# Retention into a bilinear FFN on one core: the SP queue, one stretch and two copies of the opening blocks in another order

## The chip, the cores and the metric

The kernel runs on one core of a Trainium2 chip. The metric is device time in microseconds (us). Seven runs of the kernel before gave a median of 334.33 us, from 333.03 to 336.23. One further execution was taken with the hardware profiler: it took 333.72 us, 332.0 of them inside the profiled span, at a granted TensorE clock of 1.0.

## The reference

Two stages, of which the second eats the first:

```
scores = (q @ k^T) / sqrt(64)                 # per batch (8) and head (8), 576 x 576
ret    = scores * gamma[h] ** (i - j)  for i >= j, else 0,   gamma[h] = 1 - 2 ** (-5 - h)
attn   = ret @ v                              # 8 x 8 x 576 x 64
x      = attn with heads side by side         # 4608 tokens x 512
out    = ((x @ w_a) * (x @ w_b)) @ w_out      # 512 -> 1536 -> 512, float32
```

There is no softmax, so the retention is computed block by block with running states (sums of k^T v), and the powers of gamma are folded into v (factor gamma^-j) and into the result (factor gamma^i).

## The kernel before, in words

**Pairs of key tiles.** The 4608 tokens are cut into 18 pieces of 256 tokens, called pairs here. Pairs 0 to 2 are worked in two halves of four heads each ("steps", lines 281 to 421) with transposes on TensorE. Pairs 3 to 17 are worked whole by these functions:

- `load_pair(n)` (line 134) issues six loads on SP's queue: two each of q, k and v, 256 KB each, in rows of 64 floats (256 bytes). Each of the three goes to a tile of the pool `stage`, which has four buffers for each of q, k and v.
- `ahead(n)` (line 433) turns q and k to bf16 on GpSimd (POOL) with three copies each (lines 440 and 444) and then scales v (line 445).
- `turn(n)` (line 466) issues two transposing DMAs on SP's queue (line 471), one for q and one for k. Pair 3 alone is transposed on TensorE (`turned`).
- `stretch(into, outof)` (line 620) is TensorE's share of retention, four runs of 32 small products, about 0.3 to 0.4 us each: for the pair `outof`, results from the states (line 589); for the pair `into`, its own k^T v (line 506) and its scores (line 563), which need the transposed tile; then, again for `outof`, results from the keys (line 602). The work that follows on VectorE (DVE) and ScalarE (ACT) is put into the list `later` and handed out one piece at a time by `pop()`: sums of states (lines 523 and 526), their bf16 copies (lines 530 to 537), the scaling of the result into x (line 612) and the masking of the scores (line 572). A stretch first flushes what is left in `later`. The result tile and the score tile of a stretch have one PSUM buffer each, so a stretch can't write them before the DVE work of the one before has read them.

**The FFN.** `ffn_block` (line 667) runs over blocks of tokens: 512, 256, 256 and then seven of 512. For each of the 12 slices of the hidden width it makes four products with `w_a` (line 682), copies the sum to bf16 on ACT (line 690), makes four products with `w_b` (line 697) and multiplies on DVE (line 702). Then, for every 128 tokens, 12 products with `w_out` (line 716), a copy of the sum from PSUM to a tile `osb` in SBUF (line 725 on ACT, line 727 on DVE), and a store of it. All PSUM tiles of the FFN, and two of a stretch, come in turn from one pool of four buffers (`ps_ffn`), and `osb` comes in turn from four buffers. So the copy of the sixth 128 tokens goes to the buffer of the second 128 tokens, and it needs the stores of the second to have landed. The tokens of pairs 0 to 2 are stored by two DMAs of 64 rows each (line 653).

**Who sets the order.** The schedule is written by hand. A list `todo` (lines 838 to 862) holds functions with due times, counted in products of 512 columns: the first block lasts from 0 to 144, the next two from 144 to 216 and from 216 to 288. The generator of the FFN yields the cost of each product, and an entry is called at the first allowed place ("edge") at or after its due time; in the output products these places are every four products. Each engine then works through its own queue strictly in order. SP's queue carries all q, k and v loads, all transposing DMAs and all stores, so each of them stands behind whatever was issued before it.

The parts of the order that the change touches are, in SP's queue before: the six loads of pair 5; the two stores of the first 128 tokens; the transposes of pair 4; the six stores of the other 384 tokens of the first block; the four loads of q and k of pair 6; the transposes of pair 5; the two loads of v of pair 6; two stores; the transposes of pair 6.

Of the kernel before, what the change touches and what calls it, by code (L numbers as in the profile page):

```python
# [18 lines left out]
def kernel(  # L19
# [27 lines left out]
    FIRST = 3  # L47
# [3 lines left out]
    def regular(n):  # L51
        return n - (n > NP - 3)
# [4 lines left out]
    def rows_of(n):  # L57

        if n not in LEFT:
            m = regular(n)  # L60
            return [(kp, 0, 128, m // 2, 256 * (m % 2) + 128 * kp)
                    for kp in (0, 1)]
        return [(i // 2, 64 * (i % 2), 64, 4 * LEFT[n] + i, S - 64)
                for i in range(4)]
# [43 lines left out]
    def x_of(t0, n):  # L108

        b0 = 0  # L110
        for n_b in blocks:
            if t0 < b0 + n_b:
                break
            b0 += n_b
        if b0 not in x_tiles:
            x_tiles[b0] = x_pool.tile([128, HP, 512], BF16, tag="x", name="xT")
        return x_tiles[b0][:, :, t0 - b0:t0 - b0 + n]
# [14 lines left out]
    paired = {}  # L132

    def load_pair(n, which=(0, 1, 2)):
        if n >= NP:
            return
        paired.setdefault(n, [])
        for i in which:
            name, src = (("qf", q), ("kf", k), ("vf", v))[i]
            t = stage.tile([128, 2 * DM], FP32, tag=name, name=name + "2")  # L140
            for kp, r0, m, b, s0 in rows_of(n):
                nc.sync.dma_start(
                    t[r0:r0 + m, kp * DM:(kp + 1) * DM]
                    .rearrange("p (h d) -> p h d", h=H),
                    src[b, :, s0:s0 + m, :].rearrange("h s d -> s h d"))
            paired[n].append(t)

    def load_step(n, hh, which):

        if n not in paired:  # L150
            paired[n] = [stage.tile([128, 2 * DM], FP32, tag=name, name=name)
                         for name in ("qf", "kf", "vf")]
        nc.sync.dma_start(
            paired[n][which][:, hh * DM:(hh + 1) * DM]
            .rearrange("p (h e) -> p h e", h=4),
            (q, k, v)[which][n // 2, 4 * hh:4 * hh + 4,
                             256 * (n % 2):256 * (n % 2) + 256, :]
            .rearrange("h (p two) d -> p h (two d)", two=2))

    STEPS = [(0, 0), (1, 0), (0, 1), (1, 1), (2, 0), (2, 1)]  # L160
    Q, K, V = 0, 1, 2
# [105 lines left out]
    def pop():  # L267
        if later:
            later.pop(0)()
# [163 lines left out]
    def ahead(n):  # L433


        qf, kf, vf = paired.pop(n)
        qkb = nat.tile([128, 2, 2 * DM], BF16, tag="qkb", name="qkb2")
        vb = nat.tile([128, 2 * DM], BF16, tag="vb", name="vb2")
        for w, t in ((0, qf), (1, kf)):
            nc.gpsimd.tensor_copy(qkb[0:64, w], t[0:64])  # L440
            to = qkb[64:128, w].rearrange("p (j r d) -> p j r d", r=2, d=D)
            fro = t[64:128].rearrange("p (j r d) -> p j r d", r=2, d=D)
            for r in (0, 1):
                nc.gpsimd.tensor_copy(to[:, :, 1 - r], fro[:, :, r])  # L444
        nc.gpsimd.tensor_tensor(  # L445
            vb.rearrange("p (k h d) -> p k h d", k=2, h=H),
            vf.rearrange("p (k h d) -> p k h d", k=2, h=H),
            vs2[:, 2 if n in LEFT else regular(n) % 2].unsqueeze(3).to_broadcast([128, 2, H, D]),
            op=ALU.mult)
        natural[FIRST + n, "pair"] = (qkb, vb)  # L450
# [194 lines left out]
    def store(u, cols, osb):  # L645
        n, u = place(u // 2), u % 2
        for kp, r0, m, b, s0 in rows_of(n):
            rows = out[b * S + s0:b * S + s0 + m, cols]
            if kp != u:
                continue  # L650
            if n < FIRST:
                for par in (0, 1):
                    nc.sync.dma_start(rows[par::2], osb[half(par), cols])  # L653
            else:
                nc.sync.dma_start(rows, osb[r0:r0 + m, cols])
# [11 lines left out]
    def ffn_block(tb, tok0, n, runs):  # L667

        xT = x_of(tok0, n)
        hT = h_pool.tile([128, NF, 512], BF16, tag="h", name="hT")  # L670
        f0 = 0
        for count in runs:
            has = {}
            for F in range(f0, f0 + count):
                fs = slice(F * 128, (F + 1) * 128)
                pa = (begun[F] if tb == 0 and F in begun else
                      ps_ffn.tile([128, 512], FP32, tag="ab", name="pa"))
                for c in range(NC):
                    if tb == 0 and (F, c) in begun:
                        yield n / 512, False  # L680
                        continue
                    nc.tensor.matmul(pa[:, 0:n], wa_sb[:, c, fs],  # L682
                                     xT[:, c],
                                     start=(c == 0), stop=(c == NC - 1))
                    if c < NC - 1:
                        yield n / 512, False
                if n == 512 and tb:
                    pop()
                ha = ha_pool.tile([128, 512], BF16, tag="ha", name="ha")
                nc.scalar.copy(ha[:, 0:n], pa[:, 0:n])  # L690
                has[F] = ha
                yield n / 512, False
            for F in range(f0, f0 + count):
                fs = slice(F * 128, (F + 1) * 128)
                pb = ps_ffn.tile([128, 512], FP32, tag="ab", name="pb")
                for c in range(NC):
                    nc.tensor.matmul(pb[:, 0:n], wb_sb[:, c, fs],  # L697
                                     xT[:, c],
                                     start=(c == 0), stop=(c == NC - 1))
                    if c < NC - 1:  # L700
                        yield n / 512, False
                nc.vector.tensor_tensor(hT[:, F, 0:n], has[F][:, 0:n],  # L702
                                        pb[:, 0:n], op=ALU.mult)
                pop()
                yield n / 512, True
            f0 += count
        for u in range(n // 128):
            final = tok0 + (u + 1) * 128 == NTOK
            osb = o_pool.tile([128, DM], FP32, tag="osb", name="osb")
            for part in range(2 if final else 1):  # L710
                cols = (slice(part * DM // 2, (part + 1) * DM // 2) if final
                        else slice(0, DM))
                po = ps_ffn.tile([128, 512], FP32, tag="ab", name="po")
                width = cols.stop - cols.start
                for F in range(NF):
                    nc.tensor.matmul(po[:, 0:width],  # L716
                                     hT[:, F, u * 128:(u + 1) * 128],
                                     wo_sb[:, F, cols],
                                     start=(F == 0), stop=(F == NF - 1))
                    if F in (2, 5, 8):  # L720
                        pop()
                    if F < NF - 1:
                        yield width / 512, F % 4 == 3
                if (u + part) % 2 == 0:
                    nc.scalar.copy(osb[:, cols], po[:, 0:width])  # L725
                else:
                    nc.vector.tensor_copy(osb[:, cols], po[:, 0:width])  # L727
                store(tok0 // 128 + u, cols, osb)
                pop()
                yield width / 512, True  # L730
# [75 lines left out]
    nc.sync.dma_start(gate, wo_sb[0:1, 3, 0:64])  # L806
    for i, which in ((4, Q), (4, K), (4, V), (5, Q), (5, K), (5, V)):
        load_step(*STEPS[i], which)
    for n in range(FIRST, FIRST + 3):
        load_pair(n)  # L810

# [20 lines left out]
    def turn_step(i):  # L834
# [3 lines left out]
    todo = [(8, state_step, (1, (1,))), (20, state_step, (3, (1,))),  # L838
            (100, early_casts, ()), (112, turn_step, (4,)),
            (112.1, cast_step, (5, Q, "act")), (116, score_step, (4,)),  # L840
            (124, turn_step, (5,)), (124.1, state_step, (4, (0, 1))),
            (128, score_step, (5,)), (132, output_step, (4,)),
            (132.1, state_step, (5, (0, 1))), (140, output_step, (5,))]
    todo += [(28 + 6 * step, pair_tables, (step,)) for step in range(13)]
    todo += [(170, stretch, (3, None)), (197, stretch, (4, 3)),
             (246, stretch, (5, 4)), (280, stretch, (6, 5)),
             (372, stretch, (7, 6)), (408, stretch, (8, 7))]
    for n in range(8, NP, 2):
        todo += [(starts[n] - 116, stretch, (n + 1, n)),
# [3 lines left out]
    casts = {3: 104, 4: 104.1, 5: 143, 6: 200, 7: 250, 8: 330}  # L853
    turns = {4: 104.2, 5: 151, 6: 210, 7: 338, 8: 345}
    loads = {7: 212, 8: 271, 9: 345.1, 10: 345.2}
    todo += [(150, load_pair, (6, (0, 1))), (152, load_pair, (6, (2,)))]
    for n in range(9, NP):
        casts[n], turns[n] = placed[n] - 70, placed[n] - 38
    todo += [(156 + 3 * part, turned, (3, part)) for part in range(4)]
# [45 lines left out]
```

## Time and profile before

| what | value |
|---|---|
| median of 7 runs | 334.33 us |
| the profiled execution | 333.72 us, span 332.0 us |
| TensorE products (PE) | 319.5 us busy, 96% of the span |
| DVE, ACT, POOL | 163.8, 128.4 and 114.6 us busy |
| DMA | 50.37 MB in 143175 packets, mean 152 GB/s |
| queue q1 (SP's) | 138384 packets, 45.10 MB, 65.2% of 16 engines |
| block 0 (512 tokens), from its first product to its last output product | 18.2 to 54.0 us |
| blocks 1 and 2 (256 tokens each) | 54.0 to 73.7 and 73.7 to 93.7 us |
| block 3 begins | 95.03 us |

Times inside the profile are microseconds from the span's start. A line of a timeline gives start, length, engine, line of the kernel, operation, output and inputs; "x4" is how many instructions were merged into it, and a bracket at its end says how long the engine sat idle before it and who released it. For SP's queue the length is that of issuing, not of the transfer; the time from issue to landing is asked for separately. The releaser of a wait is inferred: when the engine named was done long before, it was another, often a DMA.

### The profile page before, as it was taken

To read this page: it belongs to the slowest core of one execution; us is meant where nothing else is said; L and a number is where in the kernel's file an instruction comes from. 1 tells how busy PE (TensorE), PEld (TensorE's weight loads), DVE (VectorE), ACT (ScalarE), POOL (GpSimd) and SP (SyncE) were. 2 spreads that over 40 slices of the span, in tenths; PEclk is the share of its full clock that TensorE was granted. 3 is DMA by queue.
4 is the path that set the end of the run, shared out by engine and by line. 5 is a ranking of instruction groups with operands and counts; after the bars stand their busy time and mean duration, and the time that the engine had idled before them with its cause. 6 is when DMAs were issued, how large, how long until landed. Compare 5 with 4: busy or idle time off the path is not lost.

```text
span 332.0 us, 8671 instructions
## 1 busy us (share of the span) xinstructions
PE 319.5 (96%) x3612; PEld 167.8 (51%) x3648; DVE 163.8 (49%) x292; ACT 128.4 (39%) x275; POOL 114.6 (35%) x146
## 2 busy tenths in 40 slices
PE   8999999989989999999999999999999999999996
PEld 4644457858634554545454545454445444444443
DVE  6744445664673465656265625662456246414321
ACT  7725833553533344343235313532332333213321
POOL 4960178725258277356054505360430000000000
PEclk9999999999999999999999999999999999999999
DMA  7999999979999999994599258945850420031013
GB/s 216 251 186 207 262 227 210 204 155 219 160 206 254 222 198 217 223 213 94 138 226 208 64 128 185 220 77 149 179 118 4 137 55 0 2 95 34 1 27 100
DMA packets 143175, 50.37 MB, mean 152 GB/s; under 512 B 124576, under 2 KB 138656, under 8 KB 143136
## 3 DMA queue, kind: packets, MB, share of 16 engines
q1 hardware_dynamic: 138384, 45.10, 65.2%
q0 software_dynamic: 4752, 4.72, 8.8%
q8 instruction: 28, 0.46, 0.6%
q14 instruction: 11, 0.09, 0.1%
HBM read 37.75 MB, written 9.44 MB: 142 GB/s over the span
## 4 chain that ended last, share of the span: by engine, by line
PE 90%; DMA 4%; DVE 2%; issue 2%; SPq 1%; ACT 1%; POOL 0%; ACTq 0%; DVEq 0%; POOLq 0%
PE pb L697 27%; PE po L716 27%; PE pa L682 26%; PE o L589 2%; PE o L602 1%; DMA vf<-in_v_dram 1%; PE sc L563 1%; DMA qf<-in_q_dram 1%; PE kv L359 1%; PE kv L506 1%; DMA qkT<-qkb 1%; PE tp L316 1%; SPq L653 1%; DVE sums L526 1%; PE sc L331 1%
## 5 line engine op out<-in xcount | busy, mean ns | idle before, releaser
L702 DVE TENSOR_TENSOR hT<-ha,pb 128x512 bf16<-128x512 bf16 (+1 forms) x120 | 75.8, 633 | 100.2 <-PE pb L697 95.8
L690 ACT CAST ha<-pa 128x512 bf16<-128x512 f32 (+1 forms) x120 | 64.8, 543 | 123.4 <-PE pa L682 122.2
L697 PE MATMUL pb<-xT,wb_sb 128*128 128x512 bf16 (+1 forms) x474 | 111.5, 357 | 0.4
L682 PE MATMUL pa<-xT,wa_sb 128*128 128x512 bf16 (+1 forms) x459 | 108.4, 357 | 2.8 <-DVE xT L612 1.4
L716 PE MATMUL po<-wo_sb,hT 128*128 128x512 bf16 (+1 forms) x430 | 95.0, 373 | 1.8 <-issue 1.6
L697 PEld LDWEIGHTS <-wb_sb 128*128 128x128 bf16 x480 | 46.8, 98 | 46.4 <-issue 0.3
L682 PEld LDWEIGHTS <-wa_sb 128*128 128x128 bf16 x474 | 45.5, 98 | 46.7 <-issue 1.9
L716 PEld LDWEIGHTS <-hT 128*128 128x128 bf16 x444 | 42.3, 98 | 46.8
L440 POOL CAST qkb<-qf 64x1024 bf16<-64x1024 f32 x15 | 15.4, 1030 | 84.5 <-DMA qf<-in_q_dram 81.6
L445 POOL TENSOR_TENSOR vb<-vf,vs 128x1024 bf16<-128x1024 f32 x15 | 28.5, 1901 | 15.1 <-DMA vf<-in_v_dram 11.4
L727 DVE COPY osb<-po 128x512 f32<-128x512 f32 (+1 forms) x18 | 12.2, 676 | 41.0 <-PE po L716 40.9
L725 ACT COPY osb<-po 128x512 f32<-128x512 f32 (+1 forms) x19 | 10.9, 574 | 45.2 <-PE po L716 39.0
L526 DVE TENSOR_TENSOR sums<-kv,sums 128x256 f32<-128x256 f32 x46 | 19.5, 423 | 2.8 <-PE kv L506 0.8
L612 DVE TENSOR_TENSOR xT<-o,qs 128x512 bf16<-128x512 f32 x30 | 19.6, 682 | 2.2 <-PE o L602 2.2
L572 DVE TENSOR_TENSOR sT<-sc,mask 128x512 bf16<-128x512 f32 x30 | 19.4, 680 | 0.0
L444 POOL CAST qkb<-kf 64x512 bf16<-64x512 f32 x30 | 17.6, 614 | 0.9
L444 POOL CAST qkb<-qf 64x512 bf16<-64x512 f32 x30 | 17.6, 614 | 0.6
L440 POOL CAST qkb<-kf 64x1024 bf16<-64x1024 f32 x15 | 15.5, 1033 | 4.8 <-DMA kf<-in_k_dram 4.2
L530 ACT CAST states<-sums 64x512 bf16<-64x512 f32 x26 | 16.0, 617 | 0.3
L740 PE MATMUL w<-ones 128*128 128x256 bf16 (+1 forms) x36 | 8.2, 354 | 1.5 <-DVE ones L197 1.5
L299 POOL CAST qkb<-kf 128x512 bf16<-128x512 f32 x5 | 3.1, 614 | 18.9 <-DMA kf<-in_k_dram 18.9
L563 PE MATMUL sc<-qkT 64*64 64x64 bf16 x480 | 7.1, 195 | 1.7 <-DVE sums L526 1.1
(81 smaller groups left out, 154.9 us busy)
## 6 DMA issues: line engine op xcount, KB each, us to landing
qf<-in_q_dram SPq DMA_DIRECT2D x32, 256.0 KB, 4.8
kf<-in_k_dram SPq DMA_DIRECT2D x32, 256.0 KB, 5.0
vf<-in_v_dram SPq DMA_DIRECT2D x32, 256.0 KB, 5.3
out_dram<-osb SPq DMA_DIRECT2D x25, 256.0 KB, 2.2
out_dram<-osb SPq DMA_DIRECT2D x22, 128.0 KB, 2.4
wo_sb<-in_moe_w_out_dram POOLq DMA_DIRECT2D x3, 512.0 KB, 16.6
qf<-in_q_dram SPq DMA_DIRECT2D x8, 128.0 KB, 3.3
kf<-in_k_dram SPq DMA_DIRECT2D x8, 128.0 KB, 3.5
```

The costliest lines, as they stand in the source:

```text
L440: nc.gpsimd.tensor_copy(qkb[0:64, w], t[0:64])
L444: nc.gpsimd.tensor_copy(to[:, :, 1 - r], fro[:, :, r])
L445: nc.gpsimd.tensor_tensor(vb.rearrange("p (k h d) -> p k h d", k=2, h=H), vf.rearrange("p (k h d) -> p k h d", k=2, h=H), vs2[:, 2 if n in ...
L526: nc.vector.tensor_tensor(sums[:, i], own, prev, op=ALU.add)
L530: nc.scalar.copy(to(half(1 - r)), fro(half(r)))
L572: nc.vector.tensor_tensor(sT[:, on].rearrange("p c k s -> p (c k) s"), sc[:, on].rearrange("p c k s -> p (c k) s"), mask3.unsqueeze(1).to_ ...
L612: nc.vector.tensor_tensor(x_of(t0, 128).rearrange("p c (a s) -> p c a s", a=2), o[:, :, :, kp].rearrange("p a c s -> p c a s"), qs[:, :, s ...
L682: nc.tensor.matmul(pa[:, 0:n], wa_sb[:, c, fs], xT[:, c], start=(c == 0), stop=(c == NC - 1))
L690: nc.scalar.copy(ha[:, 0:n], pa[:, 0:n])
L697: nc.tensor.matmul(pb[:, 0:n], wb_sb[:, c, fs], xT[:, c], start=(c == 0), stop=(c == NC - 1))
L702: nc.vector.tensor_tensor(hT[:, F, 0:n], has[F][:, 0:n], pb[:, 0:n], op=ALU.mult)
L716: nc.tensor.matmul(po[:, 0:width], hT[:, F, u * 128:(u + 1) * 128], wo_sb[:, F, cols], start=(F == 0), stop=(F == NF - 1))
```

## The change

In SP's queue, `turn(4)` now stands ahead of the loads of pair 5's v, and these, with the loads of pair 6's k and q, stand ahead of the six remaining stores of the first block. The entry that loaded q and k of pair 6 at 150 is gone; v of pair 6 stays at 152. `load_pair` keeps a dictionary so that the three tensors of a pair can be loaded in any order. `stretch(6, 5)` is due at 266 instead of 280: it is called after four of the 24 output products of block 2 and no longer after sixteen. In the blocks of 256 tokens every copy of an output sum goes to ACT, where one of two went to DVE.

```diff
-        paired.setdefault(n, [])
+        paired.setdefault(n, {})
...
-            paired[n].append(t)
+            paired[n][i] = t
...
-        qf, kf, vf = paired.pop(n)
+        qf, kf, vf = (paired[n].pop(i) for i in (Q, K, V))
...
-                if (u + part) % 2 == 0:
+                if n == 256 or (u + part) % 2 == 0:
                     nc.scalar.copy(osb[:, cols], po[:, 0:width])
                 else:
                     nc.vector.tensor_copy(osb[:, cols], po[:, 0:width])
...
-    for n in range(FIRST, FIRST + 3):
+    for n in (FIRST, FIRST + 1):
         load_pair(n)
+    load_pair(FIRST + 2, (Q, K))
...
-             (246, stretch, (5, 4)), (280, stretch, (6, 5)),
+             (246, stretch, (5, 4)), (266, stretch, (6, 5)),
...
-    todo += [(150, load_pair, (6, (0, 1))), (152, load_pair, (6, (2,)))]
+    todo += [(104.3, load_pair, (5, (V,))), (104.4, load_pair, (6, (K,))),
+             (112.2, load_pair, (6, (Q,))), (152, load_pair, (6, (V,)))]
```

## The prediction, made before the changed kernel had run

> **What bounds the kernel now.** I read the page's first part, then the waits of TensorE, then the timelines of TensorE, SP's queue, ACT and DVE from 54 to 96 us, the stretch that the change touches.
>
> ```profile
> PE 319.5 (96%) x3612; PEld 167.8 (51%) x3648; DVE 163.8 (49%) x292; ACT 128.4 (39%) x275; POOL 114.6 (35%) x146
> ```
>
> TensorE is the bound of the whole, so only a wait of TensorE that goes or comes moves the end. Its timeline has three waits of over 0.3 us between products, and all lie here:
>
> ```profile
> 69.57 0.45 PE L563 MATMUL sc<-qkT 64*64 64x64 bf16 x32 [1.08 <-DVE sums L526]
> ...
> 73.67 0.60 PE L682 MATMUL pa<-xT,wa_sb 128*128 128x256 bf16 x4
> ...
> 82.06 0.45 PE L563 MATMUL sc<-qkT 64*64 64x64 bf16 x32 [0.61 <-DMA qkT<-qkb]
> ...
> 95.03 1.02 PE L682 MATMUL pa<-xT,wa_sb 128*128 128x512 bf16 x4 [1.38 <-DVE xT L612]
> ```
>
> Together 3.07 us. The first names DVE, but the scores of pair 4 read the transposed tile; its two DMAs issue at 64.22 and 65.76 and land 3.8 us after issue, the second at 69.5. So it is a wait for them. The second is for those of pair 5, the third for DVE's scaling of pair 5's result. After 95 us TensorE waits at most 0.27 us at a time. What the transposes wait for is seen in SP's queue:
>
> ```profile
> 54.19 2.38 SPq L142 DMA_DIRECT2D qf<-in_q_dram  x2
> 56.67 2.58 SPq L142 DMA_DIRECT2D kf<-in_k_dram  x2
> 59.36 3.27 SPq L142 DMA_DIRECT2D vf<-in_v_dram  x2
> 62.72 1.40 SPq L653 DMA_DIRECT2D out_dram<-osb  x2
> 64.22 3.46 SPq L471 DMA_TRANSPOSE qkT<-qkb  x2
> 67.77 5.05 SPq L653 DMA_DIRECT2D out_dram<-osb  x6
> 72.87 1.32 SPq L142 DMA_DIRECT2D qf<-in_q_dram  x2
> 74.23 1.89 SPq L142 DMA_DIRECT2D kf<-in_k_dram  x2
> 76.24 3.87 SPq L471 DMA_TRANSPOSE qkT<-qkb  x2
> ```
>
> There is no gap over 0.1 us: the queue itself is the bound, and a place in it is a time.
>
> **The change, part by part.** All is the same up to 59.36.
>
> Transposes of pair 4. They no longer stand behind the v load (3.27 us): two stores, then the transposes, so they issue by 61 to 62.5 and land, 3.8 us after the second, by 66 to 67.5. TensorE wants them at 68.49. GpSimd finished their source at 58.5. The wait of 1.08 goes: everything after is 1.06 us sooner (0.02 for the semaphore), block 2 begins at 72.6.
>
> Transposes of pair 5. The same DMAs stand ahead of them as before, in another order, so they issue again near 76.2. They landed at 82.01; TensorE will now be there at 81.45 - 1.06 = 80.4. Right ahead of them are small stores instead of four loads, and the first of the two took 2.53 us to issue where others take 1.25, so 81.0 is possible; 82.0 is the upper end. Alone, this gives back 0.6 to 1.6 of what was won.
>
> The six stores. Now v of pair 5 (moved) and four loads of pair 6 are ahead of them. The waits written into the two programs show what that touches: the copy of the sixth 128 tokens (second of block 1) waits for the stores of the second 128 tokens, the first two of the six, and no other of the six matters soon. Before, they issued at 67.77, landed at 70.8, and the copy followed its products:
>
> ```profile
> 67.77 5.05 SPq L653 DMA_DIRECT2D out_dram<-osb  x6
> ```
> ```profile
> DMA to landing us min/median/max: 2.4/2.4/2.5
> ```
> ```profile
> 73.88 0.69 DVE L727 COPY osb<-po 128x512 f32<-128x512 f32 x1 [0.98 <-PE po L716]
> ```
>
> (the middle line is the landing of just those two). Now: the stores, transposes and v loads are the six DMAs that took from 59.36 to 67.67 before, so they end near 67.7 again. Then four loads. Their own row before is 3.26 us (72.87 to 76.13), after stores; loads three to six of an unbroken run took 4.30 (111.98 to 116.28), and at the head of the stretch four took 5.06 (54.19 to 59.25). In the new place they are loads three to six of a run, so 4.3. In addition, the packet records of the instruction queue show fetches of 16 KB at 49.2, 59.1, 65.6, 71.0 and 83.6, each beside a stretched issue (the store at 70.99 took 1.83 us where others took 0.54 to 0.59); one falls near 70 and now meets these loads, about +0.8. The second store issues at 67.7 + 4.3 + 0.8 + 0.6 = 73.4 and lands 2.4 us later with the queue empty, 3.7 behind loads (the two stores at 62.7). I take 2.7, because two or three loads are still on their way at 200 GB/s: 76.1. The ends are 67.7 + 3.3 + 0.6 + 2.4 = 74.0 and 67.7 + 5.1 + 0.8 + 0.6 + 3.7 = 77.9.
>
> [...]
>
> What waits with it. The copy stands on ACT now, ahead of the eight bf16 copies of block 2, and ACT is in order. ACT is free for it at about 72.8 (line 530 ended at 73.87, 1.06 sooner). It starts at 76.15, takes 0.59 like others of line 725, and ends at 76.75. TensorE goes on meanwhile: in the program order it is the second `w_b` group of block 2 whose PSUM buffer is the one being copied. Three groups of 0.44 from 72.6 bring it to 73.9; then it waits until 76.8: **2.9 us**. Ends: 0.8 (landing 74.0) and 4.7 (77.9). GpSimd isn't behind this: pair 6's casts wait for q, whose landing moves from 77.6 to about 75.5.
>
> The scores of pair 5 come at 80.4 + 2.9 = 83.3, when their transposes have landed: no wait there. That is 83.3 - 82.06 = 1.24 later than before.
>
> The stretch of pair 6. Twelve products (12 x 0.216 = 2.6 us) move behind it. TensorE would reach it at 87.9 on the clock of before. But it needs DVE to have masked pair 5's scores, as one PSUM tile serves both, and DVE works without a break from 83.85:
>
> ```profile
> 88.08 1.28 DVE L572 TENSOR_TENSOR sT<-sc,mask 128x512 bf16<-128x512 f32 x2
> ```
>
> so the scores start at 89.41, not at 87.9 plus two runs of 0.35. From there: scores 0.45, keys 0.27, a start of 0.16, and 20 products x 0.216 = 4.33: block 3 at 94.62, where it began at 95.03, and x is ready by 92.5. The move is worth 0.41 and not 1.38. It also needs pair 6's v scaled on GpSimd (ended 88.31, wanted at 88.6) and pair 6's transposes: they landed at 91.07, and with scores at 89.41 + 1.24 = 90.65 they must come 0.4 sooner. They stand behind the same DMAs as before; each took 5.2 us to land beside two fetches, others took 3.1 to 4.7, so I expect 88 to 90 and charge nothing; the bounds are 0 and 1.
>
> Copies on ACT. Besides the wait, DVE loses two copies of 0.69 and ACT gains two of 0.59; at the end of block 2 DVE had its copy at 93.69 just ahead of the scaling that TensorE waited for, which is inside the 0.41. Later work is only shifted: loads 7 and 8 keep their places.
>
> Sum against the profiled execution: +1.24 - 0.41 = +0.8, so 333.72 becomes 334.5. The median stands 0.61 above that execution, so I forecast 334.33 + 0.8 = **335.1 us**.
>
> **Rivals.** (A) The stores land by about 74.5, the wait is 1.3 us or less. For it: stores with an empty queue land in 2.4 us. Against it: six loads in a row in front. Then the scores of pair 5 start with their transposes at 81.0 to 82.0, and block 3 begins 0.4 to 1.5 us sooner than before: 332.9 to 333.9. (B) All three waits go as the edits read, 3.07 us: 331.3. Against it: DVE's masking holds the stretch of pair 6 even then (0.41 instead of 1.38), and v of pair 6 was scaled only at 88.31. More than 1.67 us of gain needs the store, pair 5's transposes and pair 6's v all a microsecond sooner. (C) Slower beyond doubt: the same copy, with the stores landing after 77.0. Then the wait is over 3.75 us and the sum over +1.67; at 77.9 it is +2.6, 336.9. For it: the stores at 62.7, which also followed six loads, took 3.7 us; against it: the six moved DMAs gave the queue slack at 66 to 68 (102 and 132 GB/s).
>
> **How the numbers follow.** A measurement of this kernel can tell about 0.5%, 1.67 us. My forecast, a wait of 1.4 to 3.75 us, has 0.50; A 0.14; B, or any gain over 1.67, 0.07; C, with pair 6's transposes late by a microsecond as its other form, 0.29. My forecast and A lie within 0.5%: 0.64. The likeliest case's own range is 333.8 to 336.0. To leave out no more than 2 in 10 the range goes from inside A, 333.2, to C's upper end, 336.9.
>
> **What would show it.** In the timeline of the changed kernel: the scores of pair 4 without a wait at 68.5; the first copy of line 725 after the convert of pair 4 with a bracket of some 3 us that names a DMA or nothing useful; a wait of TensorE near 74 in the second `w_b` group of block 2; no wait at the scores of pair 5; a wait of about half a microsecond ahead of the scores of pair 6, released by DVE; none ahead of block 3. If ACT doesn't wait for the stores, the sum's largest term is wrong and it is A or B. If DVE's masking comes sooner relative to the scores of pair 5, the 0.41 is too small.

## The result, and the profile after

The changed kernel took 337.74 us in the median of 14 runs (335.99 to 338.89), the kernel before 334.08 us in 33 runs. The medians differ by 3.66 us; the ratio of the runs is 1.0096, with a 95% interval of 1.0072 to 1.0119, about 3.2 us. So the change made the kernel slower, by more than the range given allowed (up to 336.9), and on the side to which 0.29 had been given. The profiled execution took 338.77 us, with a span of 337.0 us and a mean granted TensorE clock of 0.995.

The page's first part and its row of the granted clock, changed kernel:

```profile
PE 321.7 (95%) x3611; PEld 169.2 (50%) x3648; DVE 162.3 (48%) x290; ACT 129.3 (38%) x277; POOL 114.6 (34%) x146
...
PEclk9999999997999999999999999999999999999999
```

TensorE is busy 2.2 us longer than before with the same products, and the clock has a dent in the tenth slice. Neither was in the forecast. The timeline of TensorE, changed kernel:

```profile
68.53 0.45 PE L563 MATMUL sc<-qkT 64*64 64x64 bf16 x32
...
72.66 0.60 PE L682 MATMUL pa<-xT,wa_sb 128*128 128x256 bf16 x4
73.09 0.60 PE L697 MATMUL pb<-xT,wb_sb 128*128 128x256 bf16 x4
73.53 0.60 PE L682 MATMUL pa<-xT,wa_sb 128*128 128x256 bf16 x4
77.60 0.60 PE L697 MATMUL pb<-xT,wb_sb 128*128 128x256 bf16 x4 [3.47 <-ACT osb L725]
...
79.72 1.06 PE L697 MATMUL pb<-xT,wb_sb 128*128 128x256 bf16 x4
80.58 1.06 PE L682 MATMUL pa<-xT,wa_sb 128*128 128x256 bf16 x4
81.43 1.06 PE L697 MATMUL pb<-xT,wb_sb 128*128 128x256 bf16 x4
...
85.55 0.63 PE L563 MATMUL sc<-qkT 64*64 64x64 bf16 x32
...
91.92 0.21 PE L589 MATMUL o<-qkT,states 64*64 64x64 bf16 x1 [0.38 <-DVE xT L612]
92.70 0.44 PE L589 MATMUL o<-qkT,states 64*64 64x64 bf16 x31 [0.56 <-ACT states L530]
...
98.62 1.03 PE L682 MATMUL pa<-xT,wa_sb 128*128 128x512 bf16 x4
```

The wait of 1.08 us at pair 4's scores is gone and block 2 begins at 72.66 instead of 73.67. The wait in the second `w_b` group stands where it was forecast, with 3.47 us. From 78.91 four groups of four products take 0.81 to 0.86 us each where the others take 0.44. The scores of pair 5 wait for nothing; ahead of the stretch of pair 6 there are two waits, 0.38 and 0.56. Block 3 begins at 98.62, where it began at 95.03.

ACT's timeline, changed kernel: the copy that waits for the stores. Before, it was on DVE at 73.88 and followed its products.

```profile
71.60 1.25 ACT L530 CAST states<-sums 64x512 bf16<-64x512 f32 x2
76.97 0.58 ACT L725 COPY osb<-po 128x512 f32<-128x512 f32 x1 [4.12 <-DMA out_dram<-osb]
```

SP's queue, changed kernel, from the first stores to pair 5's transposes:

```profile
58.65 3.17 SPq L653 DMA_DIRECT2D out_dram<-osb  x2
61.92 2.77 SPq L471 DMA_TRANSPOSE qkT<-qkb  x2
64.73 2.34 SPq L142 DMA_DIRECT2D vf<-in_v_dram  x2
67.12 1.88 SPq L142 DMA_DIRECT2D kf<-in_k_dram  x2
69.04 2.33 SPq L142 DMA_DIRECT2D qf<-in_q_dram  x2
71.48 5.76 SPq L653 DMA_DIRECT2D out_dram<-osb  x6
77.34 2.68 SPq L471 DMA_TRANSPOSE qkT<-qkb  x2
```

The stores start at 71.48 and the second lands at 76.87. Busy time by stretches, changed kernel; the number after POOL's is the granted clock:

```profile
78.00:80.00 2.00, 2.00 (x16) 1.59 (x15) 1.12 (x3) 0.51 (x3) 1.88 (x4) 0.73 0.94 187
80.00:82.00 2.00, 2.00 (x11) 1.45 (x10) 0.42 (x1) 0.67 (x2) 0.92 (x2) 0.50 0.80 149
82.00:84.00 2.00, 2.00 (x19) 1.71 (x18) 0.84 (x2) 0.58 (x3) 0.00 (x0) 0.91 1.25 269
```

In the kernel before all three have 1.00. TensorE ran at half its clock from about 78.9 to 82.3: the six groups from 78.47 to 82.76 took 4.29 us where six of 0.4375 take 2.63, so 1.67 us were lost.

Up to block 3 that accounts for the loss of 3.59 us. The profiled span grew by 5.0 us; the other 1.44 us are one wait for "issue" (a wait for nothing that the profile shows) at 128.87, where the kernel before had 0.16 us at 123.84. The line of the changed kernel:

```profile
128.87 1.46 PE L716 MATMUL po<-wo_sb,hT 128*128 128x512 bf16 x6 [1.60 <-issue]
```

This wait is not shown to belong to the change.

The 14 runs split by their clock. Two kept a clock of 1.000 and had spans of 334.3 and 334.4 us; the other twelve had 0.989 to 0.995 and spans of 335.4 to 337.2, with a median of 336.15. The difference, 1.8 us, is about the size of the dent. The kernel before has such runs too, but fewer: of its 85 runs that were taken beside the experiments, ten had a clock of 0.993 to 0.995, at 335.7 to 339.3 us. Its profiled execution kept 1.00 and had no wait over 1.38 us there, so which hole those ten had is not on record.

### The profile page after: what moved, and what is told of

It reads as the page before. It is cut to its first block, busy times and chain, and to the rows that moved or that the text cites. A ratio compares the mean times of both kernels' runs of the same rounds, so it can differ in the third digit from the quotient of the medians.

```text
span 337.0 us, 8670 instructions
## 1 busy us (share of the span) xinstructions
PE 321.7 (95%) x3611; PEld 169.2 (50%) x3648; DVE 162.3 (48%) x290; ACT 129.3 (38%) x277; POOL 114.6 (34%) x146
## 3 DMA queue, kind: packets, MB, share of 16 engines
q1 hardware_dynamic: 138384, 45.10, 64.2%
## 4 chain that ended last, share of the span: by engine, by line
PE 92%; DVE 2%; issue 2%; ACT 1%; DMA 1%; SPq 0%; ACTq 0%; DVEq 0%
PE pb L697 28%; PE pa L682 27%; PE po L716 26%; PE w L740 2%; PE o L589 2%; PE o L602 1%; PE sc L563 1%; PE kv L506 1%; PE kv L359 1%; PE tp L316 1%; DMA out_dram<-osb 1%; PE sc L331 1%; PE o L409 1%; DVE sums L526 0%; PE pa L664 0%
## 5 line engine op out<-in xcount | busy, mean ns | idle before, releaser
L725 ACT COPY osb<-po 128x512 f32<-128x512 f32 (+1 forms) x21 | 12.1, 575 | 51.8 <-PE po L716 44.8
L727 DVE COPY osb<-po 128x512 f32<-128x512 f32 (+1 forms) x16 | 10.8, 674 | 41.4 <-PE po L716 41.4
L339 DVE TENSOR_TENSOR sT<-sc,mask_s 128x1024 bf16<-128x1024 f32 x6 | 7.3, 1221 | 2.5 <-PE sc L331 2.5
```

## The experiments

My theory after the result had two terms: the copy waits for stores that pair 6's loads push back, and the hole in TensorE's work, when it is long enough, costs the clock as well. Against it stood that the loads, the earlier stretch or the copies on ACT are harmful in themselves. The opening of the kernel differs by up to 2 us between executions, so waits are compared, not places in time.

### The copy without its wait

```diff
-            osb = o_pool.tile([128, DM], FP32, tag="osb", name="osb")
+            osb = (qs_o[:, 0] if (tb, u) == (1, 1) else
+                   o_pool.tile([128, DM], FP32, tag="osb", name="osb"))
```

> The changed kernel, but the second copy of block 1 goes to a table that is no longer used (qs_o), so it needs no store to have landed. Nothing else is different. Theory (the copy's wait for the stores is what costs): ACT's wait of 4.12 us and TensorE's of 3.47 us near 74 are gone, the granted clock stays at 1.00 from 78 to 83 us (it was 0.73 and 0.50 for 78 to 80 and 80 to 82). Transposes of pair 5, which landed at 82.1, then hold the scores of pair 5 to about 82.1 as before, and block 3 begins near 95.2: ratio to the kernel before 0.997 to 1.002. Rival (the loss comes from the moved loads themselves, the stretch called sooner or the copies on ACT): the ratio stays at 1.006 or more.

Measured: 336.85 us, ratio 1.007 (1.003 to 1.0111). The theory was wrong about the time. ACT's and TensorE's waits near 74 are gone, but TensorE then came to pair 5's scores ahead of their transposes. The timeline of TensorE of this kernel:

```profile
75.86 0.60 PE L697 MATMUL pb<-xT,wb_sb 128*128 128x256 bf16 x4
...
85.81 0.62 PE L563 MATMUL sc<-qkT 64*64 64x64 bf16 x32 [3.48 <-DMA qkT<-qkb]
...
87.61 1.06 PE L697 MATMUL pb<-xT,wb_sb 128*128 128x256 bf16 x4
```

There is a hole of the same length, and the clock falls after it as well. Block 1 began 1.9 us later in this execution, so the transposes, issued at 79.36 against 77.34 us, were only 0.1 us later by that measure; but the scores that they release began 6.45 us after that issue, where in the changed kernel the second had landed 4.7 us after it, at 82.08. Why they were late is not shown. Eight of the ten runs had a lower clock (0.990 to 0.995), so the profiled execution is not an exception. The two whose clock stayed at 1.000 had spans of 332.7 and 332.8, 0.7 us above the 332.0 of the kernel before. So the first hole stood in front of a second one; taking it away alone is not enough.

### The hole filled with work

Sixteen products whose result nobody reads stand where TensorE waits.

```diff
+                if (tb, F) == (2, 1):
+                    w = ps_sc.tile([128, 2, 512], FP32, tag="sc", name="w2")
+                    for _ in range(16):
+                        nc.tensor.matmul(w[:, 0], ones[:, 0:128], ones,
+                                         start=True, stop=True)
                 pb = ps_ffn.tile([128, 512], FP32, tag="ab", name="pb")
```

> The changed kernel with 16 products of 128x512 ahead of the second w_b group of block 2, where TensorE waits 3.47 us; they write a score tile that nobody reads before it is written anew. At 0.216 us each they fill 3.46 us. Theory (the idle time lowers the clock, and that costs another 1.7 us): the copy's wait stays, the granted clock stays at 1.00 from 78 to 83 us, the groups of block 2 after the wait take 0.44 us and not 0.85, and the time falls by 1.5 to 1.8 us against the changed kernel: ratio to the kernel before 1.003 to 1.006. Rival (the products after the wait are slow because DMA traffic or weight loads disturb them): groups of 0.85 us stay, and the ratio is 1.009 or more.

Measured: 335.56 us, ratio 1.0054 (1.0028 to 1.008), about 1.4 us below the changed kernel's 1.0096 (the two intervals just touch). Eleven of its twelve runs kept a clock of 0.998 or more, where two of the changed kernel's 14 did. TensorE's timeline, and below it the clock by stretches, of this kernel:

```profile
73.86 3.62 PE L698 MATMUL w<-ones 128*128 128x512 bf16 x16
77.31 0.60 PE L702 MATMUL pb<-xT,wb_sb 128*128 128x256 bf16 x4
77.75 0.60 PE L682 MATMUL pa<-xT,wa_sb 128*128 128x256 bf16 x4
78.19 0.60 PE L702 MATMUL pb<-xT,wb_sb 128*128 128x256 bf16 x4
```
```profile
78.00:80.00 2.00, 2.00 (x21) 1.80 (x19) 1.08 (x3) 0.75 (x2) 1.88 (x4) 1.00 1.01 191
80.00:82.00 2.00, 2.00 (x20) 1.80 (x19) 1.03 (x3) 0.87 (x3) 0.41 (x1) 1.00 0.93 190
```

ACT's copy still waits (3.73 us), the second `w_b` group begins nearly as late as in the changed kernel (77.31 against 77.60), and the groups after it take 0.44 us. Adding useless work made the kernel faster: this tells the clock from the wait.

The profiles of this kernel's variants show which holes the clock fell after: with one of 1.39 us the clock stayed at 1.00, with those of 3.47, 3.48, 3.61 and 4.31 us it fell to 0.50, for 3.4 us in the first three kernels and for twice that in the last. The time of the fall was not the same in all: with the hole of 4.31 us it came 2.6 us after the hole began, in the others 3.5 to 4.8 us after. In the profile of the second kernel with stores on GpSimd's queue (below), TensorE was idle for 3.62 us between 68 and 74, 2 us of it, 70 to 72, without a break, and the clock stayed at 1.00, while eight of the twelve runs of that kernel had a lower one (0.990 to 0.995). So the runs of one kernel went either way; how long the holes were in runs without a profile is not on record.

### Copies back on DVE

```diff
-                if n == 256 or (u + part) % 2 == 0:
+                if (u + part) % 2 == 0:
```

> The changed kernel with the copies of the 256-token blocks as before: the second of each block on DVE. Theory (which engine copies is of no account, since the PSUM buffer is what the second w_b group of block 2 needs): DVE waits for the stores instead, TensorE waits 3.3 to 3.7 us at the same place, the clock drops likewise, ratio to the kernel before 1.006 to 1.013. Rival (ACT being blocked, with the bf16 copies behind the waiting one, is what makes it costly): TensorE's wait falls under 1.5 us and the ratio under 1.004.

Measured: 337.86 us, ratio 1.0101 (1.0054 to 1.0148). Now DVE waits 4.80 us for the same stores and TensorE 4.31 us in the same place:

```profile
79.69 1.01 PE L697 MATMUL pb<-xT,wb_sb 128*128 128x256 bf16 x4 [4.31 <-DVE osb L727]
```

The wait is longer than expected (3.3 to 3.7) by 0.6 us, and the clock falls, from 78.0 to 84.8. The loss is there whichever engine copies; six runs can't tell whether its size differs.

### Two loads fewer ahead of the stores

```diff
-             (112.2, load_pair, (6, (Q,))), (152, load_pair, (6, (V,)))]
+             (150, load_pair, (6, (Q,))), (152, load_pair, (6, (V,)))]
```

> The changed kernel, but the two q loads of pair 6 stand behind the six stores again (at 150), so two loads fewer stand ahead of the stores. Theory (two terms: the wait itself, and a lower clock only if the wait is long): the stores of the second 128 tokens land 2.0 to 2.5 us sooner, near 74.5, TensorE waits 1.0 to 1.6 us in the second w_b group of block 2, the clock stays 1.00 through 78 to 84 us, pair 5's transposes land near 82: ratio to the kernel before 0.999 to 1.004. Rival (time lost does not go by the length of that wait): 1.007 or more.

Measured: 334.01 us, ratio 1.0001 (0.9973 to 1.0028). TensorE's timeline:

```profile
75.88 0.60 PE L697 MATMUL pb<-xT,wb_sb 128*128 128x256 bf16 x4 [1.39 <-ACT osb L725]
```

With two loads moved away, 2.1 us of waiting are gone (3.47 to 1.39), the clock stays at 1.00, and pair 5's scores wait for nothing. Not all of it is the time of the two loads: the first store was issued at 70.28, 1.2 us sooner, and the six took 4.83 us to issue and not 5.76; the copy that needs the second began at 75.24, 1.73 us sooner. As expected, by both terms: 2.1 us of wait and 1.7 us of clock are 3.8 us, and the two ratios lie 0.95% apart, 3.2 us, within their intervals.

### The parts alone

```diff
 # pair 4's transposes ahead of pair 5's v load
-    for n in range(FIRST, FIRST + 3):
+    for n in (FIRST, FIRST + 1):
         load_pair(n)
+    load_pair(FIRST + 2, (Q, K))
...
+    todo += [(104.3, load_pair, (5, (V,))),
```

> The kernel before with one edit: the transposes of pair 4 ahead of pair 5's v load; loads of pair 6, stretch and copies as before. Theory (the queue gives back what it gains): the wait of 1.08 us at pair 4's scores is gone, the one at pair 5's scores grows from 0.61 to about 1.6 us, since the same DMAs stand ahead of their transposes, and block 3 begins within 0.3 us of before: ratio 0.998 to 1.001. Rival (the gain is kept): the wait at pair 5's scores stays under 0.9 us, ratio 0.996 to 0.9975.

Measured: 333.43 us, ratio 0.9973 (0.9948 to 0.9998), inside the rival's range, though the interval reaches into mine. The wait at pair 4's scores is gone, the one at pair 5's is 1.01 us where it was 0.61, so the queue gave back 0.4 of 1.08 us, less than the 1.0 that I had expected, and a little more than the rival's 0.3.

```diff
 # the copies of the 256-token blocks on ACT
-                if (u + part) % 2 == 0:
+                if n == 256 or (u + part) % 2 == 0:
```

> The kernel before with one edit: all copies of the 256-token blocks on ACT. The stores that the second copy of block 1 needs land at 70.8 and its products end at 73.7, so it waits for nothing. Theory (harmless alone): TensorE's waits of 1.08 and 0.61 us stay, the one ahead of block 3 falls by up to 0.69 us, since DVE's copy stood ahead of the scaling there: ratio 0.997 to 1.001. Rival (the copy holds up ACT's bf16 copies, and TensorE with them): a new wait of over 0.3 us at the start of block 2, ratio 1.002 or more.

Measured: 332.55 us, ratio 0.9978 (0.9954 to 1.0002). The wait ahead of block 3 fell from 1.38 to 0.76 us, about what DVE's copy had taken there; no wait appeared at the start of block 2. The wait at pair 4's scores was 1.28 us in this execution, and the one at pair 5's, which was expected to stay, is gone; why is not shown.

```diff
 # the stretch of pair 6 sooner
-             (246, stretch, (5, 4)), (280, stretch, (6, 5)),
+             (246, stretch, (5, 4)), (266, stretch, (6, 5)),
```

> The kernel before with one edit: the stretch of pair 6 due at 266 and not at 280. Theory (what it takes off the wait ahead of block 3, it puts in front of its own small products): the wait of 1.38 us ahead of block 3 goes; instead TensorE waits ahead of the stretch for DVE's scaling and ACT's copies of pair 5's states, about 0.4 + 0.6 us as in the changed kernel, and for pair 6's transposes, which land near 91.1 in the kernel before, where TensorE is at the scores about 89.7. Then block 3 begins 0 to 1.2 us later than before: ratio 0.999 to 1.004. Rival (the edit gains what the prediction gave it or more): 0.41 us or more won, ratio 0.9955 to 0.9985.

Measured: 334.09 us, ratio 1.0012 (0.9978 to 1.0046). The timeline of TensorE has the exchange in full: the wait ahead of block 3 is gone, three others stand in the stretch, 1.85 us together.

```profile
87.74 0.21 PE L589 MATMUL o<-qkT,states 64*64 64x64 bf16 x1 [0.38 <-DVE xT L612]
88.52 0.44 PE L589 MATMUL o<-qkT,states 64*64 64x64 bf16 x31 [0.56 <-ACT states L530]
...
90.13 0.45 PE L563 MATMUL sc<-qkT 64*64 64x64 bf16 x32 [0.91 <-DMA qkT<-qkb]
```

Five of its twelve runs had a lower clock (0.993 to 0.995, 334.6 to 336.7 us); the profiled one kept 1.00, so their hole is not on record. None of the 60 runs of the kernels with two loads fewer, with pair 4's transposes alone, with the copies on ACT alone and of the two kernels of the last section below fell under 0.998.

### The stores on GpSimd's queue

If SP's queue is what everything stands in, six stores fewer in it should help. First in the changed kernel, then with only pair 4's transposes kept of the change.

```diff
             if n < FIRST:
+                on = nc.gpsimd if n < 2 and (n, u) != (0, 0) else nc.sync
                 for par in (0, 1):
-                    nc.sync.dma_start(rows[par::2], osb[half(par), cols])
+                    on.dma_start(rows[par::2], osb[half(par), cols])
```

> The changed kernel, but the six stores of the first block that stood behind pair 6's loads are issued by GpSimd, ahead of its casts for pair 5, where it was idle. Theory (SP's queue is what both holes come from: the copy's stores and pair 5's transposes stand in it): the stores land by 70, no copy waits, pair 5's transposes issue near 71 to 73 and land by 79, so neither hole of TensorE of 3.5 us is there and the granted clock stays 1.00; block 3 begins at 92.5 to 94: ratio to the kernel before 0.991 to 0.997. Rival (the DMA engines and not the queue are the bound): the transposes land after 81 as before and the ratio is 0.998 or more.

> As the kernel with the six stores on GpSimd, but of the change only the place of pair 4's transposes is kept: pair 6's loads come at 150, its stretch at 280, copies as before. Theory: with the six stores out of SP's queue all three transposes come in time, the waits of 1.08 and 0.61 us go and the one of 1.38 us ahead of block 3 stays, since DVE's order there is that of before: block 3 at 93.0 to 93.8, ratio 0.993 to 0.997, and the earlier stretch and the copies on ACT are worth 0.2 to 1.0 us more where the queue is no bound. Rival (the earlier stretch is worth nothing even then): the two kernels with stores on GpSimd are within 0.1% of each other.

Measured: 337.79 us, ratio 1.011 (1.0075 to 1.0145), and 336.36 us, ratio 1.0076 (1.0049 to 1.0103). Both were expected to be faster than the kernel before and both are slower. The copy's wait is gone in the first, but TensorE's timeline has a hole in a place where the changed kernel had none:

```profile
72.58 0.45 PE L563 MATMUL sc<-qkT 64*64 64x64 bf16 x32 [3.61 <-DMA qkT<-qkb]
```

Here are the stores on GpSimd and pair 4's transposes on SP's queue, from the same kernel:

```profile
60.74 3.22 POOL L654 DMA_DIRECT2D out_dram<-osb  x6
```
```profile
61.88 6.14 SPq L471 DMA_TRANSPOSE qkT<-qkb  x2
```

GpSimd issued the stores from 60.74 to 63.96, beside pair 4's transposes on SP. The two transposing DMAs took 6.14 us to issue, and the scores that they release began at 72.58, 4.56 us after the issuing had ended; in the changed kernel the issuing took 2.77 us, and the second landed 3.5 us after its end. My reading is that the stores which I had taken out of the way in one queue got into it again in the DMA engines (the profile of the changed kernel counts SP's queue and GpSimd's against the same 16, 64.2% and 8.6%); that the transposes are late because of that is argued from these times, not tried. The second kernel is idle for 3.62 us between 68 and 74, where the first is for 3.93, its hole and 0.33 us after it. So the theory that the queue alone is the bound is wrong for this stretch; the six stores did well to come late. The earlier stretch with the copies on ACT was expected to be worth 0.2 to 1.0 us here; the kernel that has them, and pair 6's loads ahead too, is the slower of the two, by 0.3% with overlapping intervals, so no gain of theirs shows.

### The harmless parts together, and one more place in the queue

Pair 4's transposes ahead of v and the copies on ACT, with pair 6's loads and stretch as before:

> The two parts of the change that were faster alone, together: pair 4's transposes ahead of pair 5's v load, and the copies of the 256-token blocks on ACT; pair 6's loads behind the stores, its stretch at 280. Theory (the harm is in pair 6's loads ahead of the stores): no wait at pair 4's scores, 1.0 to 1.6 us at pair 5's, 0.7 to 0.8 ahead of block 3, clock 1.00: ratio to the kernel before 0.994 to 0.9975, no worse than either alone (0.9973 and 0.9978). Rival (the two gains are one and the same, or the transposes of pair 5 take both back): 0.998 or more.

Measured: 332.64 us, ratio 0.9961 (0.9935 to 0.9988): no wait at pair 4's scores, 1.05 us at pair 5's, 0.76 ahead of block 3. Then pair 5's transposes in front of pair 6's k:

```diff
-             (150, load_pair, (6, (0, 1))), (152, load_pair, (6, (2,)))]
+             (150, load_pair, (6, (Q,))), (152, load_pair, (6, (K, V)))]
```

> As the kernel with both parts, and pair 5's transposes ahead of pair 6's k loads (q, transposes, k, v and not q, k, transposes, v). Theory (a place in SP's queue is a time): pair 5's transposes issue about 1.9 us sooner and land near 80, the wait at pair 5's scores falls under 0.4 us; pair 6's k comes 2.5 to 3.9 us later, its casts end near 84.5 and its transposes land by 91: ratio to the kernel before 0.991 to 0.995. Rival (pair 6's transposes are now late by more than what was won): a wait of over 1 us at pair 6's scores, ratio 0.997 or more.

Measured: 331.66 us, ratio 0.9929 (0.9903 to 0.9955), faster than both kernels. SP's queue and TensorE's timeline of it:

```profile
72.09 1.32 SPq L142 DMA_DIRECT2D qf<-in_q_dram  x2
73.53 3.13 SPq L471 DMA_TRANSPOSE qkT<-qkb  x2
76.71 1.33 SPq L142 DMA_DIRECT2D kf<-in_k_dram  x2
```
```profile
80.25 0.50 PE L563 MATMUL sc<-qkT 64*64 64x64 bf16 x32
...
90.18 0.45 PE L563 MATMUL sc<-qkT 64*64 64x64 bf16 x32 [0.85 <-DMA qkT<-qkb]
...
92.56 1.03 PE L682 MATMUL pa<-xT,wa_sb 128*128 128x512 bf16 x4
```

Pair 5's transposes are issued from 73.53 to 76.66, its scores, at 80.25, wait for nothing, pair 6's scores wait 0.85 us, and block 3 begins at 92.56 with no wait ahead of it.

## Why the prediction was wrong

The mechanism was right and it was named as the largest term: the copy of the sixth 128 tokens behind the stores, ACT in order, the second `w_b` group of block 2. With two of the loads moved away, 2.1 us of that wait went. Two smaller steps came true, with some luck: the wait at pair 4's scores went, but the transposes landed at 68.21 and not by 67.5, 0.3 us ahead of the scores at 68.53; and pair 5's scores found their transposes there, helped by a hole and a slow clock that had held TensorE up for longer than forecast. Three steps failed, by block 3:

- **"Three groups of 0.44 from 72.6 bring it to 73.9; then it waits until 76.8: 2.9 us."** It measured 3.47, since the second store landed at 76.87 and not at 76.1. Mis-sized by 0.6 us. The landing took what was summed (2.8 us against 2.7); the issue did not. The first store went out at 71.48, sooner than the sum's 72.8, as the queue ran 0.7 us ahead in this execution and the four loads took 4.4 us and not 5.1; but that store alone took 2.57 us to issue, with an instruction fetch at 71.4 beside it. I had put the fetch on the loads and 0.6 us on the store.
- **"The scores of pair 5 come at 80.4 + 2.9 = 83.3."** The sum let products after a hole run as they did before it. They ran at half the clock: 1.67 us, shown by the filled hole; the two runs that kept their clock fit it. This term was missing altogether, and it was the largest error. The forecast wait of 2.9 us was only 0.6 us short of the 3.47 after which the clock fell here, with bounds of 0.8 to 4.7 us around it: the upper part of the range should have held the wait plus 1.7, which is 338.6 and not 336.9.
- **"The move is worth 0.41 and not 1.38."** From pair 5's scores to block 3 it took 13.07 us, and 12.97 before: the move was worth nothing. I looked at what the scores of the stretch wait for (DVE's masking) and not at what its first run needs: pair 4's result scaled by DVE and pair 5's states copied by ACT. Those two waits, 0.94 us, came first.

0.8 + 0.6 + 1.67 + 0.5 = 3.6 us, against 3.59 us found at block 3.

Rival A (the stores in time) would not have been what it promised: with two loads fewer in front, the wait was 1.39 us, close to its 1.3, and the time was that of the kernel before and not 0.4 to 1.5 us less; with the copy freed altogether, pair 5's transposes made a hole as long in the profiled execution. Rival C had the right side and place, and lacked the clock.

## What to carry to other kernels

A load that isn't urgent, moved ahead of a store, delays whoever reuses the stored buffer: follow the store to the next writer of its buffer, and from there to the PSUM buffer that this writer has to free; here TensorE waited 3.47 us for it. On TensorE, 95% busy, a hole had a second price in these runs when it was near 3.5 us or longer: 1.7 us lost at half clock in the changed kernel, so a bound on a wait should be carried through with that step in it. Where several transfers share one queue, give the place to the one that is wanted first, one step at a time: two such steps and the copies on ACT gave 0.7%, while the change, with the first of these steps, the same copies, the earlier stretch and loads ahead that nobody yet waited for, lost 1%.

## What was not expected of the hardware

- The clock fell after TensorE had resumed, not in the hole: work began again at 77.60 and the first slow group started near 78.9. In the kernel with copies on DVE, with a hole of 4.31 us, it was at 0.50 from 78.0, before work resumed at 79.69.
- The half clock lasted 3.4 us in each of three profiles with holes of 3.47, 3.48 and 3.61 us, and 6.8 us in the one with 4.31.
- With six 128 KB stores on GpSimd's queue beside them (60.74 to 63.96), the two transposing DMAs on SP's queue took 6.14 us to issue from 61.88 on, and the scores that they release began 10.7 us after that; in the changed kernel they took 2.77 us to issue, and the second had landed 6.3 us after 61.92.
- Fetches of 16 KB on the instruction queue stand beside issues that are 0.7 to 2 us too long on SP's queue (changed kernel: 2.57 us for a store at 71.5, beside a fetch at 71.4, where the next five take 0.54 to 0.6; kernel before: 1.92 us for a transposing DMA at 65.8, beside a fetch at 65.6, where one at 78.9 takes 1.25). That they cause them is argued from the times, not tried.
